# Sparse attention and SoLU feed-forward in one kernel: the hand-written step order laid out anew, with the inverse sums moved from GpSimd to VectorE

## The chip, the cores and the metric

One core of a Trainium2 chip runs one program. The metric is the device time of one launch in microseconds; of the kernel before three runs are shown (below). The profile is of one further execution.

## The reference

```
scores = (q @ k.T) / sqrt(64)                  # 8 batches x 8 heads, 576 x 576, head_dim 64
kth    = 32nd largest score of each row
attn   = softmax(scores where scores >= kth), else 0
x      = attn @ v                              # heads side by side: 4608 tokens x 512
h      = x @ w_in                              # 4608 x 1024
solu   = h * softmax(h)
ln     = (solu - mean) / sqrt(var + 1e-6) * g_ln
out    = ln @ w_out                            # 4608 x 512
```

q, k, v are float32; w_in and w_out come as float64 and are turned into float32 on the chip.

## The kernel before

The work is cut into 32 **pairs** (one batch, two heads). A pair has nine **tiles** j of 128 rows x 576 scores: two heads times four blocks of 128 queries, and one tile for the last 64 queries of both heads. Tokens are cut into 36 tiles of 128 (four per batch, and one of the 64-token rests of two batches).

The exact 32nd largest score is found by counting. First, moments of the scores are worked out without the scores: `prep_t`, `prep_m` transpose q and k on TensorE, `prep_tc`, `prep_mc` copy them out on ScalarE (ACT), `moments` and `spread` are small bf16 products, `spread_v` and `spread_r` (VectorE, DVE) multiply and reduce them, `first_p` (GpSimd, POOL) takes a root, `first` (DVE) makes a first threshold t0. Then `scores` (L747, PE) makes the scores of the query block t, `evac` (L758, ACT) brings a tile to SBUF as X, `count0` (L766, DVE) counts the scores over t0, `second` (L774 to L781, DVE) corrects the threshold, `count1` (L789, ACT) counts again, `third` (L798 to L806, DVE) corrects again, `count2` (L821, ACT) counts and keeps the signs `sg`. In the next step of the plan the same pair is finished: `nearest` (L842, L846, DVE) finds the eight scores next to the threshold, `kth` (L859 to L874, DVE) picks the 32nd, `exps` (L853, ACT) takes exponentials E of three tiles at a time, `keep` (L883, DVE) masks one tile of E and sums it, `inverse` inverts three sums, `norm` (L898, POOL) scales one tile, `transpose_p` (L909, PE) and `transpose_last` (L929, PE) transpose it, `copy_p` (L923, ACT) and `copy_last` copy it out, `attn_v` (L958, PE) multiplies by v in three parts, `copy_v` (ACT) copies that out.

A token tile goes through `mm1` (L982, PE), `hmax` (L991, DVE), `hexp` (ACT), `solu` (DVE), `square` (ACT), `ln` (POOL), `transpose_ln` (PE), `copy_ln` (ACT), `mm2` (L1046, PE) and `store`. One of them is worked on beside each pair, a second one in three of the steps.

**What sets the order.** Every engine takes its instructions strictly in the order in which they are written. That order is made by a table: `at(time, f, ...)` gives each piece a planned time, the list is sorted by it, and each piece then adds its instructions to its engines' queues. The planned times only sort; no engine waits for a clock. A pair's plan is shifted by `STEP` from pair to pair. The first 18 `weights_step` pieces turn the weights into float32, mostly on POOL and DVE.

**Buffers.** `ps_big` has two buffers (two banks each), taken in turn by h of `mm1`, y of `spread` and the scores; `ps_tp` has two, for all transposes; `ps_o` has two, for `spread`'s tail, `attn_v` and `mm2`. X has six buffers of three tiles, three to a pair, so pair i+2 writes where pair i had its scores: `evac` of tiles 0 to 2 of pair i+2 waits for `keep` of tiles 0 to 2 of pair i, and so on by threes. In time, `keep` of pair i, the counts of pair i+1 and `evac` of pair i+2 follow each other in one step.

Of the kernel before, what the change touches and what calls it, by code (L numbers as in the profile page):

```python
# [443 lines left out]
def fast_path(  # L444
# [612 lines left out]


    todo = []
    STEP = 40.0  # L1060

    def at(time, f, *args):
        todo.append((time, len(todo), f, args))

    def pair_times(i):
        b = i * STEP
        if i == 0:
            at(b - 40, load_qk, 0)
        else:
            at(b - 30, load_qk, i)  # L1070
# [2 lines left out]
        at(b - 18.0, prep_t, i)
        at(b - 17.4, prep_m, i, "q")
        at(b - 13.9, prep_tc, i)
        at(b - 13.6, prep_mc, i, "q")
        at(b - 13.5, prep_m, i, "k")
        at(b - 13.0, prep_mc, i, "k")
        at(b - 12.9, moments, i)
        at(b - 12.4, moments_c, i)  # L1080
        at(b - 12.2, spread, i)
        at(b - 9.6, spread_v, i)
        at(b - 8.8, spread_r, i)
        at(b - 5.0, first_p, i)
        at(b - 2.5, first, i)

        for t in range(NM + 1):
            at(b - 2.6 + 1.75 * t, scores, i, t)
        for j in range(NT):
            at(b - 1.3 + 0.875 * j, evac, i, j)  # L1090
            at(b - 0.6 + 0.875 * j, count0, i, j)
            at(b + 9.0 + 0.78 * j, count1, i, j)
            at(b + 19.9 + 0.78 * j + (1.5 if j > 3 else 0), count2, i, j)
        at(b + 7.4, second, i)
        at(b + 16.6, third, i)

        b += STEP
        for g, t in enumerate((7.4, 16.8, 18.3)):
            at(b + t, exps, i, g)
            at(b + 8.35 + 4.35 * g, side, i, g)  # L1100
            at(b + 26.0 + 2.6 * g, inverse, i, g)
        at(b + 21.5, kth, i)
        for j in range(NT):
            at(b + 8.4 + 1.45 * j, nearest, i, j)
            at(b + 23.0 + 0.8 * j, keep, i, j)
            at(b + 27.0 + 0.78 * j + 0.2 * (j // 3), norm, i, j)
            at(b + 28.0 + 0.85 * j, transpose_p, i, j)
            at(b + 28.7 + 0.85 * j, copy_p, i, j)
        for part, t in enumerate((31.2, 34.6, 35.4)):
            at(b + t, transpose_last, i, part)  # L1110
            at(b + t + 0.6, copy_last, i, part)
            at(b + t + 1.2, attn_v, i, part)
        at(b + 38.0, copy_v, i, 1)
        at(b + 39.0, copy_v, i, 2)

    def token_times(n, x, stores):

        d = {"x": x, "stores": stores}
        late = n > NPAIR
# [3 lines left out]
        at(b + 13.9, hmax, d)
        at(b + 15.8, hexp, d)
        at(b + 17.2, solu, d)
        at(b + 22.2, square, d)
        at(b + 23.6, ln, d)
# [97 lines left out]
```

## Time and profile before

| | before |
|---|---|
| three runs, median (lowest to highest) | 2001.91 us (1997.06 to 2002.42) |
| the profiled execution | 1995.56 us, span 1993.4 us |
| mean granted TensorE clock | 0.831 of 2.4 GHz |
| busy: PE, DVE, ACT, POOL | 1426.5, 1219.6, 1178.4, 659.3 us |

No engine is busy for more than 72% of the span, so shares of busy time do not say what a step costs. The steps have to be looked at one by one: `second` runs once per pair and marks their beat, and within a step the waits show which engine is behind which.

### The profile page before, as it was taken

To read this page: it belongs to the slowest core of one execution; us is meant where nothing else is said; L and a number is where in the kernel's file an instruction comes from. 1 tells how busy PE (TensorE), PEld (TensorE's weight loads), DVE (VectorE), ACT (ScalarE), POOL (GpSimd) and SP (SyncE) were. 2 spreads that over 40 slices of the span, in tenths; PEclk is the share of its full clock that TensorE was granted. 3 is DMA by queue.
4 is the path that set the end of the run, shared out by engine and by line. 5 is a ranking of instruction groups with operands and counts; after the bars stand their busy time and mean duration, and the time that the engine had idled before them with its cause. 6 is when DMAs were issued, how large, how long until landed. Compare 5 with 4: busy or idle time off the path is not lost.

```text
span 1993.4 us, 21797 instructions
## 1 busy us (share of the span) xinstructions
PE 1426.5 (72%) x7043; PEld 793.5 (40%) x7043; DVE 1219.6 (61%) x2784; ACT 1178.4 (59%) x2398; POOL 659.3 (33%) x806
## 2 busy tenths in 40 slices
PE   5254156777777788877777789777777788776797
PEld 3122033444444444444444445444444444443443
DVE  3745756666667766466677656467776666578411
ACT  5443465666666666466666665566667665576321
POOL 4557542333333222333332223333222333332301
PEclk9986577788878898888887888788888888888899
DMA  3111100000000000000000000100000000000000
GB/s 82 39 43 50 38 24 19 18 25 25 24 19 24 24 13 24 24 24 25 19 23 25 18 19 18 29 24 19 24 19 20 23 19 25 24 12 12 6 14 20
DMA packets 101899, 48.68 MB, mean 24 GB/s; under 512 B 86921, under 2 KB 95121, under 8 KB 101777
## 3 DMA queue, kind: packets, MB, share of 16 engines
q1 hardware_dynamic: 101776, 47.21, 8.8%
q8 instruction: 58, 0.95, 0.2%
q14 instruction: 65, 0.52, 0.1%
HBM read 37.75 MB, written 9.44 MB: 24 GB/s over the span
## 4 chain that ended last, share of the span: by engine, by line
DVE 40%; PE 37%; ACT 10%; POOL 5%; issue 5%; DMA 2%; SPq 0%; DVEq 0%; POOLq 0%; ACTq 0%
PE s_ps L747 11%; DVE w L842 10%; DVE w L846 10%; DVE E L883 9%; PE om L958 8%; PE tp_p L909 6%; ACT X L758 5%; PE h_ps L982 3%; PE o_ps L1046 3%; PE tp_pt L929 3%; POOL E L898 2%; DVE hmax L991 2%; DVE solu L1006 2%; POOL rden L894 1%; PE ot L958 1%
## 5 line engine op out<-in xcount | busy, mean ns | idle before, releaser
L766 DVE TENSOR_SCALAR_CACHE_REDUCE junkv<-X,t 128x576 bf16<-128x576 f32 x288 | 224.9, 810 | 297.0 <-ACT X L758 295.6
L909 PE MATMUL tp_p<-ident,E 128*128 128x128 f32 x1152 | 248.8, 369 | 207.0 <-POOL E L898 200.6
L923 ACT COPY PT<-tp_p 128x512 f32<-128x512 f32 x256 | 146.3, 587 | 375.7 <-PE tp_p L909 375.3
L747 PE MATMUL s_ps<-qkT 64*128 64x288 f32 (+1 forms) x1280 | 293.2, 493 | 44.4 <-ACT X L758 43.6
L758 ACT ACTIVATE X<-s_ps 128x576 f32<-128x576 f32 x288 | 179.5, 651 | 183.0 <-PE s_ps L747 163.3
L909 PEld LDWEIGHTS tp_p<-ident,E 128*128 128x128 f32 x1152 | 172.6, 186 | 280.1 <-POOL E L898 247.4
L814 POOL TENSOR_SCALAR tt<-t 128x9 f32<-128x9 f32 x32 | 7.5, 233 | 781.2 <-DVE al L830 778.7
L898 POOL TENSOR_SCALAR E<-E,rden 128x576 f32<-128x576 f32 x288 | 260.0, 920 | 9.7
L1046 PE MATMUL o_ps<-w_out,lnT 128*128 128x512 f32 x576 | 254.9, 595 | 1.0 <-ACT lnT L1041 1.0
L883 DVE SCALAR_TENSOR_TENSOR E<-X,kth,E 128x576 f32<-128x576 f32 x288 | 245.6, 917 | 1.4
L842 DVE SCALAR_TENSOR_TENSOR w<-X,al,sg 128x576 f32<-128x576 f32 x288 | 235.4, 817 | 3.4
L821 ACT ACTIVATE sg<-X,t 128x576 bf16<-128x576 f32 x288 | 220.1, 766 | 17.7 <-DVE t L806 13.2
L789 ACT ACTIVATE junka<-X,t 128x576 bf16<-128x576 f32 x288 | 218.7, 766 | 14.5 <-DVE al L830 7.3
L982 PE MATMUL h_ps<-w_in,xTm 128*128 128x512 f32 x512 | 225.4, 593 | 0.0
L846 DVE MAX8 w<-w 128x8 f32<-128x576 f32 x288 | 219.2, 761 | 9.9
L747 PEld LDWEIGHTS s_ps<-qkT 64*128 64x128 f32 (+1 forms) x1280 | 151.5, 199 | 168.2 <-ACT X L758 139.1
L633 PE MATMUL tp_qk<-ident,km 128*128 128x128 f32 x128 | 35.6, 434 | 254.4 <-ACT qkT L623 254.4
L1046 PEld LDWEIGHTS o_ps<-w_out,lnT 128*128 128x128 f32 x576 | 109.3, 191 | 136.9 <-issue 128.8
L853 ACT ACTIVATE E<-X 128x1728 f32<-128x1728 f32 x96 | 154.1, 1639 | 0.0
L722 DVE TENSOR_TENSOR t<-mean,zs 128x9 f32<-128x9 f32 x32 | 5.4, 169 | 237.0 <-POOL zs L712 237.0
L982 PEld LDWEIGHTS h_ps<-w_in,xTm 128*128 128x128 f32 x512 | 95.3, 191 | 109.1 <-issue 109.1
L958 PE MATMUL om<-PT,vm 128*64 128x256 f32 x1024 | 132.3, 403 | 0.0
(115 smaller groups left out, 1759.0 us busy)
## 6 DMA issues: line engine op xcount, KB each, us to landing
qm<-in_q_dram SPq DMA_DIRECT2D x32, 256.0 KB, 3.3
km<-in_k_dram SPq DMA_DIRECT2D x32, 256.0 KB, 3.3
vm<-in_v_dram SPq DMA_DIRECT2D x32, 256.0 KB, 2.7
out_dram<-osb SPq DMA_DIRECT2D x32, 256.0 KB, 2.3
w_raw<-in_moe_w_in_dram SPq DMA_DIRECT2D x8, 512.0 KB, 4.0
w_raw<-in_moe_w_out_dram SPq DMA_DIRECT2D x8, 512.0 KB, 3.4
qt<-in_q_dram SPq DMA_DIRECT2D x32, 32.0 KB, 2.2
kt<-in_k_dram SPq DMA_DIRECT2D x32, 32.0 KB, 2.8
```

The costliest lines, as they stand in the source:

```text
L747: nc.tensor.matmul(out=s[:, half, 0:SH], lhsT=qkT[hd, 0, qs], rhs=qkT[hd, 1, half * SH : (half + 1) * SH], start=True, stop=True,)
L758: nc.scalar.activation(out=x_of(i, j).rearrange("p (a s) -> p a s", a=2), in_=d.pop(("s", j))[:, :, 0:SH], func=AF.Copy, scale=scale,)
L766: nc.vector.tensor_scalar(out=junk, in0=x_of(i, j), scalar1=d["t0"][:, j : j + 1], scalar2=None, op0=ALU.is_ge, op1=ALU.add, accum_out=d[" ...
L821: nc.scalar.activation(out=d["sg", j], in_=x_of(i, j), func=AF.Sign, scale=-(1.0 + 2.0**-23), bias=d["t2"][:, j : j + 1], accum_out=d["n2" ...
L842: nc.vector.scalar_tensor_tensor(out=w, in0=x_of(i, j), scalar=d["al"][:, j : j + 1], in1=d.pop(("sg", j)), op0=ALU.subtract, op1=ALU.mult,)
L846: nc.vector.max(d["w8"][:, j, :], w)
L883: nc.vector.scalar_tensor_tensor(out=e, in0=x_of(i, j), scalar=d["kth"][:, j : j + 1], in1=e, op0=ALU.is_ge, op1=ALU.mult, accum_out=den_a ...
L898: nc.gpsimd.tensor_scalar(out=e, in0=e, scalar1=st[i]["rden"][:, j : j + 1], scalar2=1.0, op0=ALU.mult, op1=ALU.mult,)
L909: nc.tensor.transpose(tp[:, c, :], p_of(i, j)[:, c * P : (c + 1) * P], ident)
L958: nc.tensor.matmul(out=o[h * D : (h + 1) * D, :], lhsT=vm[:, h, c, :] if c < NM else vt[:, h, :], rhs=rhs[0:ks, c, :], start=(c == 0), sto ...
L982: nc.tensor.matmul(out=h[:, half, :], lhsT=x[:, c, :], rhs=w_in[:, c, half * 512 : (half + 1) * 512], start=(c == 0), stop=(c == NP - 1),)
L1046: nc.tensor.matmul(out=d["o"], lhsT=d["lnT"][:, c, :], rhs=w_out[:, c, :], start=(c == 0), stop=(c == NF - 1),)
```

## The change

The constant tile `minus1` goes. `inverse` becomes an addition and a reciprocal on DVE instead of an addition and a power on POOL. `STEP` is 38 for 40, and the planned times are new throughout:

- `scores` of the next pair stand among the transposes and the products with v of the pair before, not behind all of them; `evac` accordingly stands among `copy_p`.
- `spread_v`, `spread_r` and `first` of the next pair stand among the `keep` of the pair before, not behind them; `first_p` stands ahead of the nine `norm`.
- `transpose_ln` and `copy_ln` of a token tile stand in the step of its `ln`, ahead of the scores, not in the next step behind them.
- The extra token tile of two batches has its `mm1` behind `mm2` of the regular one, 14.7 planned units later than that one's.

```diff
     def inverse(i, g):
         js = slice(3 * g, 3 * g + 3)
         rden = st[i]["rden"][:, js]
-        nc.gpsimd.tensor_scalar(
-            out=rden, in0=den_all[:, i, js], scalar1=1e-9, scalar2=1.0, op0=ALU.add, op1=ALU.mult
-        )
-        nc.gpsimd.tensor_tensor(out=rden, in0=rden, in1=minus1.broadcast_to([P, 3]), op=ALU.pow)
+        nc.vector.tensor_scalar(
+            out=rden, in0=den_all[:, i, js], scalar1=1e-9, scalar2=None, op0=ALU.add
+        )
+        nc.vector.reciprocal(rden, rden)
...
-    STEP = 40.0
+    STEP = 38.0
...
-        at(b - 9.6, spread_v, i)
-        at(b - 8.8, spread_r, i)
-        at(b - 5.0, first_p, i)
-        at(b - 2.5, first, i)
+        at(b - 10.5, spread_v, i)
+        at(b - 9.7, spread_r, i)
+        at(b - 9.0, first_p, i)
+        at(b - 6.5, first, i)
...
-            at(b - 2.6 + 1.75 * t, scores, i, t)
+            at(b - 9.0 + 1.8 * t, scores, i, t)
...
-            at(b - 1.3 + 0.875 * j, evac, i, j)
+            at(b - 7.5 + 0.9 * j, evac, i, j)
...
-            at(b + 28.0 + 0.85 * j, transpose_p, i, j)
-            at(b + 28.7 + 0.85 * j, copy_p, i, j)
+            at(b + 32.2 + 0.95 * j, transpose_p, i, j)
+            at(b + 32.8 + 0.95 * j, copy_p, i, j)
```

In the rows of the changed kernel's order below, lines are two lower than before (`scores` L745, `evac` L756 and so on).

TensorE, one step from the transposes of a pair to the token products. Before (`tp_pt` is `transpose_last`, `om` and `ot` are `attn_v`, `s_ps` is `scores`, `h_ps` and `o_ps` are `mm1` and `mm2`):

```order
L909 MATMUL tp_p<-ident,E 128x128 x16
L929 MATMUL tp_pt<-ident,E 64x128 x4
L909 MATMUL tp_p<-ident,E 128x128 x8
L958 MATMUL om<-PT,vm 64x256 x8
L958 MATMUL om<-PT,vt 64x256 x2
```

The first products with v follow here, then the rest of the transposes, all other products with v, and only then:

```order
L958 MATMUL ot<-PTt,vm 64x64 x8
L958 MATMUL ot<-PTt,vt 64x64 x2
L747 MATMUL s_ps<-qkT 128x288 x16
L747 MATMUL s_ps<-qkT 64x288 x4
L1034 MATMUL tp_ln<-ident,solu 128x128 x8
L982 MATMUL h_ps<-w_in,xTm 128x512 x8
L1046 MATMUL o_ps<-w_out,lnT 128x512 x8
```

All 20 instructions of the scores stood behind the last product with v. The same place in the changed kernel:

```order
L1032 MATMUL tp_ln<-ident,solu 128x128 x8
L745 MATMUL s_ps<-qkT 128x288 x8
L907 MATMUL tp_p<-ident,E 128x128 x4
L745 MATMUL s_ps<-qkT 128x288 x4
L907 MATMUL tp_p<-ident,E 128x128 x8
L745 MATMUL s_ps<-qkT 128x288 x4
L907 MATMUL tp_p<-ident,E 128x128 x4
L927 MATMUL tp_pt<-ident,E 64x128 x4
L907 MATMUL tp_p<-ident,E 128x128 x4
L745 MATMUL s_ps<-qkT 64x288 x4
L956 MATMUL om<-PT,vm 64x256 x8
L956 MATMUL om<-PT,vt 64x256 x2
```

Two of the five blocks of scores now stand ahead of the first transpose, the others between transposes, the last ahead of the first product with v.

ScalarE in the changed kernel, the same place (`X<-s_ps` is `evac`, `PT<-tp_p` is `copy_p`):

```order
L643 ACTIVATE qkT,mom<-tp_qk 128x512
L660 COPY mom<-tp_m 128x64
L1039 COPY lnT<-tp_ln 128x512 x2
L756 ACTIVATE X<-s_ps 128x576 x3
L921 COPY PT<-tp_p 128x4x128
L756 ACTIVATE X<-s_ps 128x576
L921 COPY PT<-tp_p 128x4x128
L756 ACTIVATE X<-s_ps 128x576
L921 COPY PT<-tp_p 128x4x128
L756 ACTIVATE X<-s_ps 128x576
L921 COPY PT<-tp_p 128x4x128
L756 ACTIVATE X<-s_ps 128x576
```

From the fourth `evac` on each stands behind a `copy_p`; before, all nine stood in one run behind the copies.

VectorE between `kth` and the counts (`yq`, `mean` and `ss` are `spread_v` and `spread_r`, `E,den_all` is `keep`, `rden` is `inverse`). Before:

```order
L874 SCALAR_TENSOR_TENSOR kth<-kth 128x9
L883 SCALAR_TENSOR_TENSOR E,den_all<-X,kth,E 128x576 x9
L692 TENSOR_TENSOR yq<-y_ps,qm 128x512
L695 TENSOR_SCALAR mean<-y_ps 128x8
L692 TENSOR_TENSOR yq<-y_t,qm 128x64
L695 TENSOR_SCALAR mean<-y_t 128x1
L703 TENSOR_REDUCE ss<-yq 128x9
```

In the changed kernel:

```order
L872 SCALAR_TENSOR_TENSOR kth<-kth 128x9
L690 TENSOR_TENSOR yq<-y_ps,qm 128x512
L693 TENSOR_SCALAR mean<-y_ps 128x8
L690 TENSOR_TENSOR yq<-y_t,qm 128x64
L693 TENSOR_SCALAR mean<-y_t 128x1
L881 SCALAR_TENSOR_TENSOR E,den_all<-X,kth,E 128x576
L701 TENSOR_REDUCE ss<-yq 128x9
L881 SCALAR_TENSOR_TENSOR E,den_all<-X,kth,E 128x576 x3
L889 TENSOR_SCALAR rden<-den_all 128x3
L892 RECIPROCAL rden<-rden 128x3
```

The first `keep` now stands behind `spread_v`, which needs the next pair's moments from PE and ACT.

## Rows read from the trace of the kernel before

**Rows 1.** The page: span, busy time, and the chain that ended last.

```profile
span 1993.4 us, 21797 instructions
PE 1426.5 (72%) x7043; PEld 793.5 (40%) x7043; DVE 1219.6 (61%) x2784; ACT 1178.4 (59%) x2398; POOL 659.3 (33%) x806
DVE 40%; PE 37%; ACT 10%; POOL 5%; issue 5%; DMA 2%; SPq 0%; DVEq 0%; POOLq 0%; ACTq 0%
```

**Rows 2.** Windows: busy time and count by engine, granted clock, DMA share, GB/s.

```profile
62.50:279.00 216.50, 83.66 (x525) 51.31 (x525) 126.62 (x284) 98.10 (x201) 125.42 (x113) 0.75 0.14 42
279.00:1808.20 1529.20, 1163.20 (x5865) 648.44 (x5866) 995.70 (x2281) 982.97 (x2010) 464.18 (x602) 0.83 0.08 21
...
1808.20:1993.40 185.20, 142.66 (x507) 71.31 (x505) 71.44 (x149) 65.92 (x121) 40.81 (x52) 0.89 0.04 12
...
951.70:1006.50 54.80, 41.15 (x216) 23.11 (x215) 36.60 (x84) 36.17 (x75) 17.00 (x22) 0.84 0.09 22
...
778.70:841.70 63.00, 50.83 (x243) 28.26 (x242) 36.45 (x84) 37.99 (x79) 16.94 (x22) 0.86 0.09 23
```

**Rows 3.** Waits over the span: who for whom, total, times, longest.

```profile
ACT PT L923 <- PE tp_p L909: 375.3, 211, 18.3
DVE junkv L766 <- ACT X L758: 295.6, 156, 15.2
```

**Rows 4.** Timeline of DVE and POOL from `keep` on, one step.

```profile
1028.19 0.82 DVE L883 SCALAR_TENSOR_TENSOR E<-X,kth,E 128x576 f32<-128x576 f32 x1
1028.93 0.08 DVE L883 DVE_READ_ACCUMULATOR E<-X,kth,E 128x1 f32 x1
...
1030.63 1.31 POOL L894 TENSOR_TENSOR rden<-rden,minus 128x3 f32<-128x3 f32 x1
1032.04 3.72 POOL L898 TENSOR_SCALAR E<-E,rden 128x576 f32<-128x576 f32 x3
1032.63 1.29 DVE L883 SCALAR_TENSOR_TENSOR E<-X,kth,E 128x576 f32<-128x576 f32 x1
1036.00 0.75 DVE L703 TENSOR_REDUCE ss<-yq 128x9 f32<-128x576 f32 x1
1037.09 2.20 POOL L898 TENSOR_SCALAR E<-E,rden 128x576 f32<-128x576 f32 x3
```

**Rows 5.** Timeline of PE in the same step: transposes, products, scores.

```profile
1034.60 2.33 PE L909 MATMUL tp_p<-ident,E 128*128 128x128 f32 x8
1043.99 1.09 PE L909 MATMUL tp_p<-ident,E 128*128 128x128 f32 x8
...
1046.84 1.95 PE L958 MATMUL om<-PT,vm 128*64 128x256 f32 x16
1049.30 0.69 PE L958 MATMUL ot<-PTt,vm 128*64 128x64 f32 x16
1050.17 1.24 PE L747 MATMUL s_ps<-qkT 64*128 64x288 f32 x8
1054.31 7.75 PE L747 MATMUL s_ps<-qkT 64*128 64x288 f32 x24 [0.27 <-ACT X L758]
```

**Rows 6.** Groups of instructions: busy us, mean ns, idle before.

```profile
L821 ACT ACTIVATE sg<-X,t 128x576 bf16<-128x576 f32 x288 | 220.1, 766 | 17.7 <-DVE t L806 13.2 <-DVE w L842 4.5
L758 ACT ACTIVATE X<-s_ps 128x576 f32<-128x576 f32 x288 | 179.5, 651 | 183.0 <-PE s_ps L747 163.3 <-ACT X L758 19.0
L853 ACT ACTIVATE E<-X 128x1728 f32<-128x1728 f32 x96 | 154.1, 1639 | 0.0
L923 ACT COPY PT<-tp_p 128x512 f32<-128x512 f32 x256 | 146.3, 587 | 375.7 <-PE tp_p L909 375.3
```

**Rows 7.** Windows of one step by stage, columns as in rows 2.

```profile
1027.00:1038.00 11.00, 5.29 (x37) 3.44 (x36) 9.65 (x26) 4.04 (x11) 7.71 (x9) 0.50 0.16 37
1038.00:1050.20 12.20, 11.87 (x95) 7.76 (x95) 0.34 (x2) 5.32 (x10) 6.74 (x10) 0.86 0.08 17
1054.30:1060.00 5.70, 5.69 (x18) 3.05 (x18) 3.30 (x9) 2.46 (x4) 0.00 (x0) 0.56 0.00 0
```

More of the change, by code (lines that the diff above doesn't have):

```diff
@@ L504, in fast_path @@
     nc.gpsimd.memset(phalf, 0.5)
-    minus1 = const.tile([P, 1], F32, tag="minus1", name="minus1")
-    nc.gpsimd.memset(minus1, -1.0)
     ones = const.tile([P, 1], F32, tag="ones", name="ones")
@@ L1066, in pair_times @@
         b = i * STEP
[L1067 to L1070, printed above, removed]
+        at(b - 32, load_qk, i)
         at(b + 1, load_v, i)
[L1073 to L1081, printed above, removed]
@@ L1082, in pair_times @@
-        at(b - 9.6, spread_v, i)
-        at(b - 8.8, spread_r, i)
-        at(b - 5.0, first_p, i)
-        at(b - 2.5, first, i)
+        at(b - 17.0, prep_t, i)
+        at(b - 16.4, prep_m, i, "q")
+        at(b - 13.0, prep_tc, i)
+        at(b - 12.8, prep_mc, i, "q")
+        at(b - 12.7, prep_m, i, "k")
+        at(b - 12.2, prep_mc, i, "k")
+        at(b - 12.1, moments, i)
+        at(b - 11.7, moments_c, i)
+        at(b - 11.5, spread, i)
+        at(b - 10.5, spread_v, i)
+        at(b - 9.7, spread_r, i)
@@ L1087, in pair_times @@
+        at(b - 9.0, first_p, i)
+        at(b - 6.5, first, i)
         for t in range(NM + 1):
-            at(b - 2.6 + 1.75 * t, scores, i, t)
+            at(b - 9.0 + 1.8 * t, scores, i, t)
         for j in range(NT):
-            at(b - 1.3 + 0.875 * j, evac, i, j)
[L1091 to L1095, printed above, removed]
+            at(b - 7.5 + 0.9 * j, evac, i, j)
+            at(b - 2.0 + 0.77 * j, count0, i, j)
+            at(b + 6.4 + 0.77 * j, count1, i, j)
+            at(b + 17.7 + 0.77 * j + (1.5 if j > 3 else 0), count2, i, j)
@@ L1097, in pair_times @@
+        at(b + 5.2, second, i)
+        at(b + 14.3, third, i)
         b += STEP
-        for g, t in enumerate((7.4, 16.8, 18.3)):
+        for g, t in enumerate((4.8, 14.6, 16.1)):
             at(b + t, exps, i, g)
-            at(b + 8.35 + 4.35 * g, side, i, g)
-            at(b + 26.0 + 2.6 * g, inverse, i, g)
-        at(b + 21.5, kth, i)
+            at(b + 6.2 + 4.26 * g, side, i, g)
+            at(b + 30.2 + 2.25 * g, inverse, i, g)
+        at(b + 23.0, kth, i)
         for j in range(NT):
-            at(b + 8.4 + 1.45 * j, nearest, i, j)
-            at(b + 23.0 + 0.8 * j, keep, i, j)
-            at(b + 27.0 + 0.78 * j + 0.2 * (j // 3), norm, i, j)
-            at(b + 28.0 + 0.85 * j, transpose_p, i, j)
-            at(b + 28.7 + 0.85 * j, copy_p, i, j)
@@ L1109, in pair_times @@
-        for part, t in enumerate((31.2, 34.6, 35.4)):
+            at(b + 6.3 + 1.42 * j, nearest, i, j)
+            at(b + 27.9 + 0.75 * j, keep, i, j)
+            at(b + 31.2 + 0.9 * j, norm, i, j)
+            at(b + 32.2 + 0.95 * j, transpose_p, i, j)
+            at(b + 32.8 + 0.95 * j, copy_p, i, j)
+        for part, t in enumerate((35.5, 39.2, 40.5)):
             at(b + t, transpose_last, i, part)
             at(b + t + 0.6, copy_last, i, part)
-            at(b + t + 1.2, attn_v, i, part)
@@ L1113, in pair_times, with token_times @@
-        at(b + 38.0, copy_v, i, 1)
-        at(b + 39.0, copy_v, i, 2)
-    def token_times(n, x, stores):
+        for part, t in enumerate((36.8, 40.6, 42.4)):
+            at(b + t, attn_v, i, part)
+        at(b + 43.0, copy_v, i, 1)
+        at(b + 43.8, copy_v, i, 2)
+    def token_times(n, x, stores, more=0.0):
         d = {"x": x, "stores": stores}
         late = n > NPAIR
-        b = (NPAIR + 1) * STEP + 15.0 * (n - NPAIR - 1) if late else n * STEP
-        c = b + 15.0 if late else b + STEP
+        b = (NPAIR + 1) * STEP + 6.0 + 15.0 * (n - NPAIR - 1) if late else n * STEP + more
@@ L1122, in token_times @@
         at(b + 6.5, mm1, d)
[L1123 to L1127, printed above, removed]
+        at(b + 14.0, hmax, d)
+        at(b + 15.4, hexp, d)
+        at(b + 17.5, solu, d)
+        at(b + 20.5, square, d)
+        at(b + 22.0, ln, d)
+        lt, c = (28.7, 30.0) if late else (27.2, STEP + 13.7 - more / 2)
         for g in range(2):
-            at(c + (13.7 if late else 5.7) + 0.3 * g, transpose_ln, d, g)
-            at(c + (13.8 if late else 6.4) + 0.4 * g, copy_ln, d, g)
@@ L1131, in token_times @@
-        at(c + 14.3, mm2, d)
-        at(c + 21.5, store, d)
+            at(b + lt + 0.3 * g, transpose_ln, d, g)
+            at(b + lt + 0.6 + 0.4 * g, copy_ln, d, g)
+        at(b + c, mm2, d)
+        at(b + c + 7.3, store, d)
     def batch_times(b):
@@ L1142, in batch_times @@
         if b % 2 == 1:
+            last = b == B - 1
             token_times(
-                n + NM if b == B - 1 else n + NM - 0.5, lambda: xs["t", b // 2],
+                n + NM - (not last), lambda: xs["t", b // 2],
                 [
@@ L1148, in batch_times @@
                 ],
+                0.0 if last else 14.7,
             )
-    at(-11.0, load_g)
+    at(-10.0, load_g)
     at(-14.0, load_w, 0)
     for n in range(len(w_chunks) + 2):
-        at(11.0 + 9.7 * n, weights_step, n)
+        at(11.0 + STEP / 4 * n, weights_step, n)
     for i in range(NPAIR):
```

## The prediction

> **What bounds the kernel now.** I read the page first: no engine is busy for more than 72% of the span, and the chain that ended last runs 40% on DVE, 37% on PE and 10% on ACT [rows 1]. So no single engine's work sets the time; a loop through several does. The windows give its beat: from the fifth `second` at 279.0 to the last at 1808.2 lie 27 steps, 1529.2 us, 56.6 each; a plain one is 54.8, with DVE busy 36.60, ACT 36.17, PE 41.15 and POOL 17.00 of it, and one with an extra token tile 63.0 [rows 2]. Every engine has 13 us or more of slack in each step. Where it lies the waits tell: ACT waits 375.3 us for transposes, DVE 295.6 us in `count0` for `evac` [rows 3]. In a step, DVE works through `nearest`, `kth` and `keep` while PE has little to do; then PE transposes and multiplies by v while DVE stands; then PE makes scores, ACT takes them out and DVE counts at that pace. Three stages in a row, DVE, then PE, then PE with ACT, and only the last of them feeds the next `nearest`. The reader should see in rows 7 that DVE is busy 0.34 of the 12.20 us of the middle stage.
>
> **The change, part by part.**
>
> *Scores among the transposes.* The step is no longer scores behind products behind transposes. I follow the new order from the end of `spread_v` (time 0) until the next one, each engine in its own order, first with the durations of full clock.
>
> (a) To the last `evac`. The first one needs the X buffer that three `keep` release; `ss` stands among them: 3 x 0.74 (start to start) + 0.75 [rows 4] = 3.0. Two `evac` of 0.65 [rows 6], the rest of the second block of scores (three quarters of it must wait for the second `evac`; a block is 1.24 [rows 5], so with some overlap 0.8), the first transpose 0.55 (1.09 for two [rows 5]) and 0.25 more until the first `norm`: 5.9. The fourth `evac` stands behind the first `copy_p` (0.59 [rows 6]) and behind the sixth `keep`, which releases its buffer at about 7.0: 7.6. Then score rest 0.85, transpose 0.55, `copy_p` 0.6, `evac` 0.65, `copy_p` 0.6, `evac` 0.65: 11.5. Score rest 0.85, transpose 0.55, and on ACT `copy_p`, `evac`, `copy_last`, `copy_p`, `evac` (3.1): 16.0. PE has the last block done at 15.4, then the first product with v, 2.46 (1046.84 to 1049.30 [rows 5]), which is 17.9; the transpose behind it, its copy, and the last `evac` 0.65: **19.7**.
>
> (b) To `count1`. Four more copies with one wait for `transpose_last`, 2.7, end at 22.4, then `exps` 1.6 [rows 6]; meanwhile PE goes through the second product from 21.6 to 24.1 and the last one, 0.87 (1049.30 to 1050.17 [rows 5]), to 25.0, and `copy_v` ends at **25.2**. DVE has done the last `count0` and `second` by 21.4.
>
> (c) `count1`, `exps`, `hexp`, `exps`, `count2`, `square`, `store`, the copies of `prep` and of the moments stand in one run on ACT. ACT's 36.17 a step [rows 2], less nine `evac` (179.5/32 = 5.6), the copies of transposes (5.2 and 1.4 for the rests), one `exps` 1.6 and four smaller copies (2.0), is 20.4; with 1.1 for gaps (an estimate) 21.5: 46.7.
>
> (d) `spread` and `spread_v`, estimated at 1.6 from their place in the step before (0.4 and 0.3 of matmuls, then 0.9 on DVE): **48.3**, and the loop closes. It is a loop of ACT and PE now. DVE has 36.60 + 1.2 for the reciprocals, and 3 for contention (below), 41 in all; it waits some 7 us at `spread_v`, with nine `keep` queued behind it. That is the wait the change adds, and POOL's `norm`, PE's transposes and the release of X wait for those nine; without it the 3.0 at the head of (a) would be over by time 0, and the loop up to 3 us shorter.
>
> *The clock.* PE's granted clock was 0.50 from 1027 to 1038, in the stretch where PE was busy 5.29 of 11.00 us, 0.86 in the denser one after it, and 0.56 in most of the scores [rows 7]. 0.50 is 1.2 GHz, 1.0 is 2.4. At the low level the transposes of two tiles took 2.33 for 1.09, three blocks of scores 7.75 for 3 x 1.24 [rows 5]. If the whole of (a) ran at it, four score rests gain 0.8 each and five transposes 0.6: 6.4, and the loop is 54.7. The new stage mixes scores, transposes and waits for ACT as the half-clock stretches of before do, but the tail of (d) and the products with v are dense. I take half of the surcharge: **51.5**, between the bounds 48.3 and 54.7.
>
> The Trainium skill speaks against the change here ("TensorE: Matmul & The Clock Gate", section "HAM oscillation — how this bites in real kernels"): short bursts of matmuls with idle time between them let the gate fall back, and each burst again starts at the lower rate. By that rule all of (a) would run at 1.2 GHz and the loop would be 54.7; the trace agrees with 0.50 and 0.56 for two such stretches, not with 0.86 for the third.
>
> *Inverse sums on DVE.* POOL loses an addition and a power per three tiles; the first power took 1.31 beside `keep` [rows 4]. The third `keep` ends 0.74 after 1028.93 and the first `norm` starts at 1032.04 [rows 4], 2.4 later. Now a `keep` more stands ahead, and two small DVE instructions of about 0.2 each. Three pairs cost DVE 1.2 a step, hidden in its 7 us of waiting; POOL's 17.00 falls by about 4, which nothing waits for. If DVE's cover were gone the price is 1.2 a step.
>
> *`norm` beside more of DVE's work.* Three `norm` took 3.72 beside `keep` and 2.20 alone; `keep` took 1.29 beside `norm` and 0.82 alone [rows 4]. Up to six `keep` run beside `norm`: 6 x 0.48 = 2.9, in the 41 above, off the path but for the release of X, where 7.0 has it. `norm` at 1.24 each keeps ahead of the transposes, which come every 1.5 to 3 us.
>
> *Token pieces.* `transpose_ln` and `copy_ln` move a step ahead into PE's wait for `moments` and `spread`; I cost them at nothing, since PE's scores wait for `keep` until 3.0. The extra token tile (three steps) holds a `ps_big` buffer that the scores need until its `solu`; it cost some 12 us before (63.0 and its neighbour, over 54.8 each [rows 2]) and I leave it at that. The loads of q and k keep their place between those of v and the store on SP, and q and k are there 20 us ahead.
>
> *The weights.* In the three steps from 62.5 to 279.0 the work on the weights has POOL busy 125.42 of 216.50 [rows 2]; that stays. I take 3.3 a step from the new order, 10, with bounds 0 and 21. *The end*, 185.2 [rows 2], is PE's token products; ahead of them the last pair's `nearest` no longer waits as long for `hmax`: 8, from 0 to 10.
>
> **The sum.** 27 x 51.5 + 36 (three extra tiles) = 1426.5, which is 102.7 less than 1529.2; with 10 and 8, 121. The profiled execution took 1995.56; the median of the runs is 2001.91, 0.3% above it. 1995.56 - 121 = 1874.6, and 0.3% more: **1881**.
>
> **The rivals.**
>
> *The clock takes it back.* All of (a) at 1.2 GHz: 27 x 54.7 + 36 = 1513, 16 less; with the 18 of weights and end 1961, as a median **1968**. For it: rows 7 and the rule. Against it: products and scores that stand close together were at 0.86. Chance 0.16.
>
> *The clock stays up.* 48.3: 27 x 48.3 + 36 = 1340, 189 less; with 18, as a median **1794**. For it: scores now fill the gaps between transposes. Chance 0.17.
>
> *Slower.* The low level lasts through the products with v as well: their 2.46, 2.46 and 0.87 double on the path of (a) and (b), 54.7 + 5.8 = 60.5, 27 x 60.5 + 36 = 1670, 140 more, as a median **2124**. It decides once the surcharge of a step is over 7.7 us ((1529.2 + 18 - 36)/27 = 56.0 against 48.3). Against it: the same products ran at full clock behind transposes before (1.95 us [rows 5]). Chance 0.07.
>
> *No change.* DVE's run of `nearest`, `kth`, `keep` still stands ahead of the transposes, and `keep` now waits for `spread_v`, so what PE no longer costs behind the transposes is lost ahead of them: about **2002**. Against it: (c) leaves DVE 7 us. Chance 0.05.
>
> **How the numbers follow.** The forecast has 0.55. Faster by over 0.3% (what these runs can tell from no change, since they spread that far): 0.55 + 0.16 + 0.17 = 0.88; same 0.05; slower 0.07. The range 1780 to 1975 takes in both clock cases and leaves out the last two and a margin at the fast end.
>
> **What would show it.** Right: `second` every 50 to 53 us; ACT with hardly an idle microsecond from `count1` to the moments; DVE's longest wait at `yq`, 5 to 8 us a step; ACT's wait for transposes well under 375; the granted clock between 0.6 and 0.9 from `spread_v` to the products. Wrong: a wait of `evac` for `keep`, or of `keep` for POOL, larger than those; `norm` late for the transposes; or a clock at one level throughout (a).

## The result, and the profile after

| | before | changed kernel |
|---|---|---|
| median (lowest to highest), 4 runs each | 2001.29 us (1997.06 to 2002.42) | 1855.62 us (1852.51 to 1857.31) |
| ratio, 95% interval | | 0.9274 (0.9255 to 0.9293) |
| span of the profiled execution, granted clock | 1993.4 us, 0.831 | 1853.2 us, 0.821 |

The changed kernel is faster by 145.7 us; 1881 had been forecast. The page after, against [rows 1]:

```profile
span 1853.2 us, 21831 instructions
PE 1478.1 (80%) x7043; PEld 822.0 (44%) x7043; DVE 1258.0 (68%) x2976; ACT 1159.3 (63%) x2398; POOL 554.0 (30%) x613
PE 48%; ACT 33%; DVE 11%; POOL 3%; DMA 2%; issue 2%; SPq 0%; DVEq 0%; ACTq 0%; POOLq 0%
```

DVE's share of the chain that ended last fell from 40% to 11%, ACT's rose from 10% to 33%: the loop now runs through PE and ACT. Windows of the changed kernel, cut at the second, fifth and last `second`, then one plain step (no extra token tile), the next, two stretches of the first one's head, and two stretches of the next one's; columns and counterparts in [rows 2]:

```profile
63.50:253.00 189.50, 91.46 (x473) 54.43 (x474) 131.51 (x300) 91.79 (x195) 111.02 (x94) 0.59 0.16 47
253.00:1682.20 1429.20, 1203.02 (x5872) 671.34 (x5870) 1024.89 (x2448) 968.45 (x2012) 383.95 (x441) 0.83 0.09 23
1682.20:1853.20 171.00, 146.67 (x556) 73.81 (x553) 75.47 (x161) 67.69 (x126) 32.13 (x40) 0.93 0.05 15
1204.40:1254.20 49.80, 41.81 (x218) 23.46 (x215) 37.80 (x91) 35.57 (x75) 13.96 (x16) 0.86 0.10 25
1254.20:1307.10 52.90, 45.62 (x217) 25.59 (x215) 37.92 (x90) 35.59 (x75) 13.95 (x16) 0.81 0.09 23
...
1228.00:1239.40 11.40, 10.24 (x53) 6.86 (x53) 8.77 (x26) 5.05 (x12) 6.16 (x6) 0.50 0.23 52
1239.40:1248.90 9.50, 7.67 (x45) 4.57 (x44) 7.40 (x20) 5.63 (x11) 5.66 (x7) 0.99 0.01 2
...
1285.00:1289.00 4.00, 3.17 (x13) 2.04 (x14) 3.93 (x12) 1.47 (x4) 3.82 (x5) 0.80 0.01 2
1289.00:1293.00 4.00, 4.00 (x12) 2.16 (x12) 3.93 (x11) 0.90 (x2) 4.00 (x5) 0.50 0.00 0
```

The 27 steps take 1429.2 for 1529.2, the three weights steps 189.5 for 216.5, the end 171.0 for 185.2. Nearly all plain steps take 49.8 to 51.2 or 53.0 to 53.2, with the same instructions in the same order. PE's timeline of two steps shows why (start, duration, engine, line, operation, tiles, shape, count, idle before). In the step of 49.8 the head runs at half clock until 1239.4 and at full clock from there; in the one of 52.9 the clock falls a second time:

```profile
1230.62 1.97 PE L1032 MATMUL tp_ln<-ident,solu 128*128 128x128 f32 x8
1232.51 2.29 PE L745 MATMUL s_ps<-qkT 64*128 64x288 f32 x8
1235.54 2.83 PE L745 MATMUL s_ps<-qkT 64*128 64x288 f32 x8 [0.73 <-ACT X L756]
...
1241.80 1.09 PE L907 MATMUL tp_p<-ident,E 128*128 128x128 f32 x8
...
1285.09 1.77 PE L745 MATMUL s_ps<-qkT 64*128 64x288 f32 x8 [0.74 <-ACT X L756]
1287.60 1.11 PE L907 MATMUL tp_p<-ident,E 128*128 128x128 f32 x4 [0.74 <-POOL E L896]
1288.65 3.58 PE L745 MATMUL s_ps<-qkT 64*128 64x288 f32 x8
1292.16 1.97 PE L907 MATMUL tp_p<-ident,E 128*128 128x128 f32 x8
```

The same two transposes take 1.09 and 1.97, a block of scores 1.77 (at 1285.09) and 3.58. The difference of the two steps, 53.0 - 49.8 = 3.2, is half of the 6.4 that the prediction gave to the whole head. The steps of 51.0 lie between the two in their granted clock as well (0.83). The two waits of [rows 3], both shorter now, and the one that the change added:

```profile
ACT PT L921 <- PE tp_p L907: 336.0, 150, 8.7
DVE junkv L764 <- ACT X L756: 232.2, 116, 4.1
DVE yq L690 <- PE y_ps L672: 130.7, 28, 6.8
```

DVE's new wait at `spread_v` is 130.7 / 28 = 4.7 us a step. A third wait shrank most, PE's for POOL's `norm`, before and in the changed kernel:

```profile
PE tp_p L909 <- POOL E L898: 200.6, 63, 17.4
...
PE tp_p L907 <- POOL E L896: 35.9, 16, 7.7
```

ACT's timeline of the step of 49.8 shows the last wait of the head and the start of `count1`:

```profile
1234.84 1.19 ACT L756 ACTIVATE X<-s_ps 128x576 f32<-128x576 f32 x2 [1.63 <-PE s_ps L745]
...
1252.13 0.59 ACT L921 COPY PT<-tp_p 128x512 f32<-128x512 f32 x1 [2.92 <-PE tp_p L907]
1252.62 0.66 ACT L756 ACTIVATE X<-s_ps 128x576 f32<-128x576 f32 x1
1258.89 0.78 ACT L787 ACTIVATE junka<-X,t 128x576 bf16<-128x576 f32 x1
```

### The profile page after: what moved, and what is told of

It reads as the page before. It is cut to its first block, busy times and chain, and to the rows that moved or that the text cites. A ratio compares the mean times of both kernels' runs of the same rounds, so it can differ in the third digit from the quotient of the medians.

```text
span 1853.2 us, 21831 instructions
## 1 busy us (share of the span) xinstructions
PE 1478.1 (80%) x7043; PEld 822.0 (44%) x7043; DVE 1258.0 (68%) x2976; ACT 1159.3 (63%) x2398; POOL 554.0 (30%) x613
## 4 chain that ended last, share of the span: by engine, by line
PE 48%; ACT 33%; DVE 11%; POOL 3%; DMA 2%; issue 2%; SPq 0%; DVEq 0%; ACTq 0%; POOLq 0%
PE s_ps L745 15%; ACT junka L787 8%; ACT sg L819 8%; PE om L956 8%; PE tp_p L907 7%; PE h_ps L980 6%; PE o_ps L1044 6%; ACT PT L921 4%; ACT E L851 3%; ACT X L756 3%; DVE E L881 3%; PE tp_pt L927 2%; DVE w L840 2%; DVE w L844 2%; PE tp_ln L1032 2%
## 5 line engine op out<-in xcount | busy, mean ns | idle before, releaser
L745 PE MATMUL s_ps<-qkT 64*128 64x288 f32 (+1 forms) x1280 | 384.4, 607 | 87.9 <-ACT X L756 55.6
L764 DVE TENSOR_SCALAR_CACHE_REDUCE junkv<-X,t 128x576 bf16<-128x576 f32 x288 | 222.9, 808 | 233.0 <-ACT X L756 232.2
L921 ACT COPY PT<-tp_p 128x512 f32<-128x512 f32 x256 | 147.4, 591 | 336.0 <-PE tp_p L907 336.0
L745 PEld LDWEIGHTS s_ps<-qkT 64*128 64x128 f32 (+1 forms) x1280 | 196.2, 255 | 233.0 <-ACT X L756 135.0
L896 POOL TENSOR_SCALAR E<-E,rden 128x576 f32<-128x576 f32 x288 | 272.6, 965 | 16.6 <-DVE rden L892 14.0
L756 ACT ACTIVATE X<-s_ps 128x576 f32<-128x576 f32 x288 | 186.1, 657 | 145.2 <-PE s_ps L745 111.9
L881 DVE SCALAR_TENSOR_TENSOR E<-X,kth,E 128x576 f32<-128x576 f32 x288 | 260.9, 937 | 0.2
L907 PE MATMUL tp_p<-ident,E 128*128 128x128 f32 x1152 | 219.8, 334 | 50.4 <-POOL E L896 35.9
L907 PEld LDWEIGHTS tp_p<-ident,E 128*128 128x128 f32 x1152 | 154.3, 168 | 143.8 <-POOL E L896 75.7
L956 PE MATMUL om<-PT,vm 128*64 128x256 f32 x1024 | 124.6, 385 | 0.0
L690 DVE TENSOR_TENSOR yq<-y_ps,qm 128x512 f32<-128x512 f32 x32 | 22.1, 691 | 140.2 <-PE y_ps L672 130.7
```

Of the source, the lines that this page charges most:

```text
L745: nc.tensor.matmul(out=s[:, half, 0:SH], lhsT=qkT[hd, 0, qs], rhs=qkT[hd, 1, half * SH : (half + 1) * SH], start=True, stop=True,)
L756: nc.scalar.activation(out=x_of(i, j).rearrange("p (a s) -> p a s", a=2), in_=d.pop(("s", j))[:, :, 0:SH], func=AF.Copy, scale=scale,)
L881: nc.vector.scalar_tensor_tensor(out=e, in0=x_of(i, j), scalar=d["kth"][:, j : j + 1], in1=e, op0=ALU.is_ge, op1=ALU.mult, accum_out=den_a ...
L896: nc.gpsimd.tensor_scalar(out=e, in0=e, scalar1=st[i]["rden"][:, j : j + 1], scalar2=1.0, op0=ALU.mult, op1=ALU.mult,)
L907: nc.tensor.transpose(tp[:, c, :], p_of(i, j)[:, c * P : (c + 1) * P], ident)
L956: nc.tensor.matmul(out=o[h * D : (h + 1) * D, :], lhsT=vm[:, h, c, :] if c < NM else vt[:, h, :], rhs=rhs[0:ks, c, :], start=(c == 0), sto ...
```

## The experiments

Each ran three rounds beside the kernel before, which took 1994 us in all of them and 2001 beside the changed kernel; so runs are compared by their ratios to it, given in brackets with the 95% interval. "Plain steps" are those without an extra token tile; "like steps" are those of two kernels that both have, or both lack, a long second low stretch of the clock. Line shifts are left out of the diffs.

**The two parts of the change alone.** `pow_back` is the changed kernel with the inverse sums on GpSimd again, `recip_alone` the kernel before with them on VectorE (its diff; `pow_back` has the reverse, and the tile `minus1` again):

```diff
-        nc.gpsimd.tensor_scalar(out=rden, ..., scalar1=1e-9, scalar2=1.0, op0=ALU.add, op1=ALU.mult)
-        nc.gpsimd.tensor_tensor(out=rden, in0=rden, in1=minus1.broadcast_to([P, 3]), op=ALU.pow)
+        nc.vector.tensor_scalar(out=rden, ..., scalar1=1e-9, scalar2=None, op0=ALU.add)
+        nc.vector.reciprocal(rden, rden)
```

> The new order with inverse put back on GpSimd (an addition and a power, as before). Theory A, the step is a loop of ACT and PE: the first norm comes some 2 us later than its present start, of which the first transpose has 1 us to spare, so about 1 us a step is lost: 1865 to 1895 us, against 1856 for the changed kernel. Theory C, the gain came from the sums' move to VectorE: more than half of it goes back, over 1930 us.

> The kernel before with nothing changed but inverse, on VectorE. In the old order the norms and the inverse sums of a pair stand in one run on GpSimd ahead of the transposes, and the three powers with their additions take some 4.5 us of it, so theory A has 1 to 3 us a step to gain: 1905 to 1970 us against 2001. Theory C has most of the whole gain here: under 1890 us. If the norms alone set the pace: 1990 to 2005.

| | time | ratio to before (95%) | weights steps / 27 steps / end | plain steps |
|---|---|---|---|---|
| before | 1994 | | 217 / 1529 / 185 | 54.8 to 55.2, 57.1 to 57.5 |
| new order, sums on GpSimd (`pow_back`) | 1937.81 | 0.9723 (0.9706 to 0.9739) | 191 / 1502 / 179 | 53.0 to 53.2, 54.1 to 55.8 |
| old order, sums on VectorE (`recip_alone`) | 1923.26 | 0.9631 (0.9595 to 0.9667) | 215 / 1462 / 181 | 52.0 to 52.8, 54.6 |
| both (the changed kernel) | 1855.62 | 0.9274 (0.9255 to 0.9293) | 190 / 1429 / 171 | 49.8 to 51.2, 53.0 to 53.2 |

By the ratios the order alone gives 2.8% (56 us), the sums alone 3.7% (71 us), the two together 7.3%: they nearly add up. `pow_back` came out in the range of theory C, `recip_alone` in that of theory A. By the columns of the 27 steps the sums, which the prediction costed at nothing, have 67 to 72 of the 100 us gained there and the order 28 to 33, whichever is put in first; the order has 25 more in the weights steps. The two waits that shrank in the changed kernel [rows 3] are longer than before in `pow_back`, so the new order by itself did not shorten them:

```profile
ACT PT L923 <- PE tp_p L909: 423.9, 146, 10.3
DVE junkv L766 <- ACT X L758: 369.0, 178, 4.1
```

PE's wait for `norm` over the span is 200.6 before, 145.3 in `recip_alone`, 95.7 in `pow_back` and 35.9 with both. POOL's timeline in `pow_back` shows where the sums stand in the new order:

```profile
1000.64 0.70 POOL L708 TENSOR_SCALAR zs<-ss 128x9 f32<-128x9 f32 x1 [6.37 <-DVE ss L703]
1001.42 2.24 POOL L712 TENSOR_TENSOR zs<-zs,phalf 128x9 f32<-128x9 f32 x1
...
1004.04 0.82 POOL L891 TENSOR_SCALAR rden<-den_all 128x3 f32<-128x3 f32 x1
1004.94 1.31 POOL L894 TENSOR_TENSOR rden<-rden,minus 128x3 f32<-128x3 f32 x1
1006.36 2.01 POOL L898 TENSOR_SCALAR E<-E,rden 128x576 f32<-128x576 f32 x2
```

And PE's, beside it:

```profile
1002.92 1.77 PE L747 MATMUL s_ps<-qkT 64*128 64x288 f32 x8 [0.74 <-ACT X L758]
1007.69 1.11 PE L909 MATMUL tp_p<-ident,E 128*128 128x128 f32 x4 [3.00 <-POOL E L898]
```

`first_p`, the sum, the power and the first `norm` follow each other on POOL, and PE stands 3.00 us for that `norm`. In the changed kernel POOL goes from `first_p` straight to `norm`, and PE's wait at the same place (1287.60, behind the block at 1285.09 above) is 0.74. The first transpose starts 4.77 after the second block of scores here (1002.92 to 1007.69) and 2.51 after it there: 2.3 of the 2.7 to 3.2 us by which like steps differ.

`inverse_early` asks what the place of the sums is worth in the old order:

```diff
-            at(b + 26.0 + 2.6 * g, inverse, i, g)
+            at(b + 25.1 + 2.4 * g, inverse, i, g)
```

> The kernel before with the inverse sums on VectorE (recip_alone, 1923 us), and each inverse right behind its third keep instead of one or two keep later; nothing else. It asks what of the 74 us between recip_alone and scores_spread_back (1850) is this place. A: the first norm starts one keep (0.8 us) earlier and the whole chain of norms, transposes and scores with it: 0.6 to 0.9 us a step, 20 to 30 us, 1893 to 1905. B: the place is worth nothing, since the norms run behind each other and the last of them comes no earlier: 1918 to 1928; the rest lies in the other differences of that layout (weights earlier, moments and token pieces in other places).

It took 1956.87 (0.9816, 0.9797 to 0.9835): neither branch, but 33.6 slower than `recip_alone`. Like steps are about as long as there (52.9 for 52.0 to 52.8, and 54.6 in both); but here nearly all plain ones are 54.6, there six. PE's timeline of such a step, from the second block of scores on:

```profile
1036.71 1.89 PE L747 MATMUL s_ps<-qkT 64*128 64x288 f32 x8 [0.73 <-ACT X L758]
1038.87 7.74 PE L747 MATMUL s_ps<-qkT 64*128 64x288 f32 x24 [0.27 <-ACT X L758]
```

And the third block in a step of 52.0 in `recip_alone`, whose later blocks stay at full clock:

```profile
1010.83 1.77 PE L747 MATMUL s_ps<-qkT 64*128 64x288 f32 x8 [0.27 <-ACT X L758]
```

Branch B's reason held for the work (the first `norm` came 0.6 earlier, the last 0.2 later, counted from `second`); the rest is the second low stretch. In like steps the sums are worth some 2.4 us a step in the old order (54.8 to 52.4, 57.2 to 54.6). The mix of step lengths moved the whole kernel by 1.8% here (0.9816 - 0.9631), half of what `recip_alone` gained, so the 71 and 56 us above are those of these layouts and carry an uncertainty of that size.

**The interleaving.** `scores_back` puts the scores, `evac` and `count0` of the changed kernel back into one run behind the last product with v (`second`, two `copy_v` and one `exps` are shifted with them):

```diff
-            at(b - 9.0 + 1.8 * t, scores, i, t)
+            at(b + 4.5 + 0.3 * t, scores, i, t)
-            at(b - 7.5 + 0.9 * j, evac, i, j)
-            at(b - 2.0 + 0.77 * j, count0, i, j)
+            at(b + 4.65 + 0.15 * j, evac, i, j)
+            at(b + 4.75 + 0.15 * j, count0, i, j)
```

> The changed kernel with scores, evac and count0 put back into one run behind the last product with v; all else as changed. Theory A: the ten microseconds and more of scores stand in the loop again while the transposes are no faster than their norms; 4 to 6 us a step more, 1950 to 2030 us. Theory C: the interleaving is worth little, under 1890 us.

It took 2100.15 (1.0532, 1.0515 to 1.055), slower than the kernel before and than every expectation: steps of 61.4. Here `keep` still stands behind `spread_v`, so moments, `keep`, `norm`, transposes, products and scores all follow one another. `scores_spread_back` also takes that away:

```diff
-            at(b - 10.5, spread_v, i)
-            at(b - 9.7, spread_r, i)
-            at(b - 9.0, first_p, i)
-            at(b - 6.5, first, i)
+            at(b - 3.9, spread_v, i)
+            at(b - 3.8, spread_r, i)
+            at(b - 0.2, first_p, i)
+            at(b - 0.1, first, i)
-            at(b + 30.2 + 2.25 * g, inverse, i, g)
+            at(b + 29.7 + 2.25 * g, inverse, i, g)
```

(and `norm` 0.9 earlier).

> scores_back, and spread_v, spread_r, first_p and first put back behind the nine keep and the norms, as in the kernel before; the sums on VectorE stay. In scores_back a step took 61.4 us, 8 more than the old order with the same sums (recip_alone). If what makes it so is that keep stands behind spread_v and the norms behind first_p while the scores no longer need them early: 52 to 55 us a step, 1890 to 1970 us. If the rest of the new order is to blame (copies, exps, token pieces): still over 2050 us.

It took 1849.88 (0.9279, 0.9264 to 0.9295), faster than either range and the time of the changed kernel by the ratios, with steps of 51.4 (53.7 with a second low stretch) and weights steps, 27 steps and end of 205, 1411 and 170. So interleaving the scores buys nothing that a serial order does not reach with the sums on VectorE: it pays back what putting `spread_v` ahead of `keep` costs. What gives this kernel another 73 us over `recip_alone` was not taken apart further; `inverse_early` shows that moving the sums forward is not enough for it.

**The head of the loop.** `keep_first` puts the first three `keep` and their sum ahead of `spread_v`:

```diff
-            at(b + 27.9 + 0.75 * j, keep, i, j)
+            at(b + (26.0 + 0.2 * j if j < 3 else 27.9 + 0.75 * j), keep, i, j)
-            at(b + 30.2 + 2.25 * g, inverse, i, g)
+            at(b + (26.9 if g == 0 else 30.2 + 2.25 * g), inverse, i, g)
```

> The changed kernel with the first three keep and the first inverse put ahead of spread_v, into VectorE's wait of 4 to 5 us for it. The three keep release the X buffers and the first norm can start earlier. Theory A, with the scores' start (token transposes and the first block at half clock) as what sets the head of the loop: 0 to 1 us a step, 1825 to 1856 us. Theory B, VectorE's wait with nine keep queued behind it is what the step now pays for: 3 us a step, 1760 to 1775 us.

1838.65 (0.923, 0.9208 to 0.9252), about 0.5% under the changed kernel and in theory A's range. `keep_ln` is that, with `transpose_ln` and `copy_ln` behind the first block of scores:

```diff
-        lt, c = (28.7, 30.0) if late else (27.2, STEP + 13.7 - more / 2)
+        lt, c = (28.7, 30.0) if late else (29.5, STEP + 13.7 - more / 2)
-            at(b + lt + 0.6 + 0.4 * g, copy_ln, d, g)
+            at(b + lt + (0.6 if late else 2.0) + 0.4 * g, copy_ln, d, g)
```

> As keep_first, and the token tile's transposes and copies moved from ahead of the first block of scores to behind it. Theory A: the scores start 1.9 us earlier and X is free by then; 1.5 to 2.5 us a step, 1785 to 1815 us. Theory B: no more than keep_first.

1784.39 (0.8953, 0.8938 to 0.8968), at the fast end of theory A's range. PE's timeline of its head:

```profile
1028.89 3.08 PE L745 MATMUL s_ps<-qkT 64*128 64x288 f32 x8
1031.90 1.97 PE L1032 MATMUL tp_ln<-ident,solu 128*128 128x128 f32 x8
...
1035.61 0.66 PE L907 MATMUL tp_p<-ident,E 128*128 128x128 f32 x4
```

The scores start right behind `spread`, where the changed kernel first spends 1.97 on `transpose_ln` at half clock; that piece now fills the 0.73 that PE waited for `evac`. The first transpose, 0.66, is already at full clock, 6.7 us after `spread`; in the changed kernel it takes 1.11 at 1238.30, 7.6 after. Nearly all plain steps are 48.2 to 49.2.

**The clock.** `warm` is meant to fill PE's wait for ACT's copies ahead of the moments: the transposes of q are made seven times over.

```diff
-        for c in range(NM):
+        for c in list(range(NM)) * (7 if nm == "q" else 1):
```

> The changed kernel with the four transposes of q repeated six times over (same tile, same values), in the 4 us in which PE waits for ACT. Theory A with the clock as a term of its own: the clock does not fall to half in that wait, and the token transposes, the first two blocks of scores and the first transpose take 1.5 to 3 us less a step: 1765 to 1815 us. If buffers and ACT set that stretch whatever the clock: 1850 to 1860 us. If the clock falls all the same the repeats outlast the wait: 1870 to 1920 us.

1874.03 (0.9393, 0.9377 to 0.9409), slower than without. Windows from the repeated transposes on, columns as above:

```profile
1289.60:1293.20 3.60, 3.56 (x31) 3.24 (x30) 3.36 (x9) 3.60 (x10) 1.74 (x3) 1.00 0.23 79
1293.20:1295.00 1.80, 0.11 (x1) 0.11 (x2) 0.20 (x1) 1.80 (x6) 0.18 (x1) 1.00 0.02 6
1295.00:1297.30 2.30, 1.44 (x24) 1.08 (x24) 0.05 (x1) 1.75 (x6) 0.00 (x0) 0.78 0.04 9
1297.30:1305.00 7.70, 6.97 (x26) 4.48 (x24) 7.63 (x22) 2.79 (x5) 5.04 (x5) 0.50 0.35 77
1305.00:1313.00 8.00, 7.63 (x24) 4.51 (x24) 7.09 (x21) 3.54 (x7) 6.75 (x8) 0.50 0.00 0
```

The repeats filled only part of the wait: behind them PE was busy for 1.55 of 4.10 us, with waits of 1.73 and 0.86 for ACT. The clock stayed at 1.00 until 1295 and fell before 1297.30, to 0.50 over all of the head, in which PE was busy for 14.60 of 15.70 us. So the low stretch came later, and the kernel was slower. The time lies in the third range, but not for its reason, since the repeats ended before the wait did; a run that leaves PE no idle time there was not made.

**Other steps of the prediction.** `extra_early` moves the extra token tile's `mm1`, `hmax`, `hexp` and `solu` forward by 5.7 planned units, `weights_late` the weights pieces back by 3, and `attn_late` moves the first product with v behind two more transposes:

```diff
+        e = 5.7 if more else 0.0
-        at(b + 6.5, mm1, d)
+        at(b + 6.5 - e, mm1, d)
...
-        at(11.0 + STEP / 4 * n, weights_step, n)
+        at(14.0 + STEP / 4 * n, weights_step, n)
...
-        for part, t in enumerate((36.8, 40.6, 42.4)):
+        for part, t in enumerate((38.2, 40.6, 42.4)):
```

> The changed kernel with the extra token tile's first product, maximum, exponential and solu 5.7 planned units earlier, so that solu stands ahead of keep and frees the PSUM buffer before the scores want it. The trace of the changed kernel has PE wait 8 us for that solu in three steps, and scores at half clock behind it: 20 to 30 us less in all, 1826 to 1836 us. If something else is as late in those steps: 1850 to 1858 us.

1837.13 (0.9207, 0.9192 to 0.9223): some 13 to 18 less than the changed kernel, short of the 20 to 30 expected. The steps of an extra tile took 58.3, 56.0 and 54.9 for 62.6.

> The changed kernel with the weights' pieces three planned units later, which puts one of four per step between the norms, as in the kernel before; the other three stay clear of them. If the early steps gained (27 us where 10 were forecast) because the norms run unbroken: 4 to 8 us in each of some four steps is lost, 1870 to 1890 us. If they gained as all other steps did: 1850 to 1862 us.

1879.86 (0.9433, 0.9417 to 0.9449), as expected if the unbroken `norm` are the cause: the weights steps rose to 211, the rest stayed at 1431 and 171. POOL's timeline in one of them:

```profile
172.93 2.59 POOL L896 TENSOR_SCALAR E<-E,rden 128x576 f32<-128x576 f32 x2
176.15 1.07 POOL L560 TENSOR_SCALAR w_out<-w_out,g_col 128x512 f32<-128x512 f32 x1 [0.63 <-DVE w_out L52]
...
186.06 5.09 POOL L896 TENSOR_SCALAR E<-E,rden 128x576 f32<-128x576 f32 x7
```

Weights work stands between the second and the third `norm`, 10 us long; in the changed kernel the nine run in one piece.

> The changed kernel with the first product with v put behind the transposes of tiles 5 and 6 (it stood between those of tiles 4 and 5). In the trace of the changed kernel ACT waits 2.9 us for the transpose of tile 5 behind that product, and the last evac and the last count0 wait with it. Theory A: PE and ACT work side by side there, 1 to 2 us a step less: 1795 to 1830 us. If the product is only moved to where the copies wait for it: 1850 to 1860 us.

1846.21 (0.9253, 0.9237 to 0.9268): the interval overlaps with the changed kernel's, and neither range holds. The 27 steps took 1431 for 1429, plain ones mostly 51.3 (50.2 to 53.4); what was gained lies in the weights steps, 181 for 190. ACT's wait behind the product fell from 2.92 to 0.90, but its waits for transposes over the span did not (336.0 in the changed kernel, 345.3 here), and the granted clock was 0.795 for 0.821. That the clock took the gain back is argued from those numbers, not shown.

> keep_ln, extra_early and attn_late together. If the three shorten different stretches of the loop, their gains add up: 1784 less 12 to 18 for the extra tiles and what attn_late shows: 1725 to 1770 us. If they shorten the same one: 1770 to 1785 us.

`all_three` (`keep_ln`, `extra_early` and `attn_late` together) took 1752.17 (0.8784, 0.877 to 0.8799), with plain steps of 47.3 to 48.4: 5.3% under the changed kernel by the ratios (0.8784 / 0.9274), the fastest version here. It lies in the range for gains that add up: 34 us under `keep_ln`, where the other two alone had given 13 and 4 (all by the ratios).

## Why the prediction was right, and where not

**The loop and its length: right.** The walk gave 51.5 a step between 48.3 and 54.7; the 27 steps took 1429.2 for 1426.5. From the end of `spread_v` at 1231.5 the last `evac` ended at 1253.3, 21.8 on (19.7 at full clock); `count1` came 5.6 behind it (5.5); ACT's run took 20.9 in the step ahead (1209.1 to 1230.0; 21.5); moments and `spread_v` 1.5 (1.6). DVE's wait stood at `yq`, if with 4.7 for 7. PE and ACT close the loop, as the chain shows. One of its signs did not come: ACT's wait for transposes is 336.0, not "well under 375"; and though DVE's longest single wait is at `yq`, those in `count0` still add up to more (232.2 us over the span, 130.7 at `yq`).

**The clock: the size right, the picture not.** The 6.4 for all of (a) is 6.2 by its own terms (4 x 0.8 and 5 x 0.6). "Half of the surcharge" is not what every step pays: the step of 49.8 has one low stretch, that of 53.0 two, and by their granted clocks (0.86 and 0.81) some 14 and 20 us at the low level. "The clock takes it back" and "stays up" were drawn as rivals for the whole run, and the kernel lies between them.

By the rule that was cited (the Trainium skill, "TensorE: Matmul & The Clock Gate", section on HAM oscillation) idle time between bursts is what lets the clock fall. The trace agrees in part: the second fall of the longer step came while PE was busy for 3.17 of 4.00 us, waiting 0.74 at a time, and the fall in `warm` behind waits of 1.73 and 0.86. That all of (a) would be low is not what it shows: 0.99 from 1239.4 on in the step of 49.8. Nor does dense work alone mean the high level: PE was busy for 4.00 of 4.00 us at 0.50 from 1289, and in [rows 7] already for 5.69 of 5.70 at 0.56, which the prediction counted among the stretches with idle time. Its "products and scores that stand close together were at 0.86" is misread too: that stretch of [rows 7] has transposes and products, and no scores. The measurement decides.

**The inverse sums: wrong.** The step that failed is "POOL's 17.00 falls by about 4, which nothing waits for". POOL's total does not limit a step, but its first power stood in series with the first `norm`, and PE's first transpose waits for that one. [Rows 4] had half of it: the power ends at 1031.94 and the first `norm` starts at 1032.04. The other half stands in PE's timeline of the kernel before, in the same step, in a row that [rows 5] leaves out:

```profile
1033.38 3.55 PE L909 MATMUL tp_p<-ident,E 128*128 128x128 f32 x12 [4.21 <-POOL E L898]
```

PE stood 4.21 us for that `norm`. The 2.4 us between third `keep` and first `norm` were read and not followed to PE. POOL's 17.00 fell by 3.0, to 13.96 a step. In runs the sums are worth 71 us in the old order, some 37 there with the step lengths of `inverse_early`, and some 90 in the new order (0.9723 - 0.9274, of 1994).

**The source of the rest: wrong.** The whole of a step's gain was credited to the scores among the transposes. With the sums costed right, the order alone has 56 us, 25 of them in the weights steps and 7 at the end, and it lengthened the waits that the interleaving was to shorten (`pow_back`); `scores_spread_back` reaches the same total with the scores in one run. The total came out because the walk took each engine's durations in the new order, whatever had made it shorter.

**Mis-sized terms.** Weights steps: 27 for 10, since nothing stands between the `norm` any more (`weights_late` gives 22 back). The end: 14.2 for 8; both lie outside the bounds given. The extra tile: 62.6 + 56.9 is 17.5 over two plain steps of 51, not 12; three times 5.5 more explains why the plain steps could be shorter than 51.5 and the sum still hold; that the two errors, some 15 us each, cancel is luck. `transpose_ln`, "at nothing": its place is worth 55 us between `keep_first` and `keep_ln` (0.923 - 0.8953, of 1994), 1.7 a step. "Up to 3 us shorter" without DVE's wait: `keep_first` found 0.5%, since the first `evac` waited 1.63 us for scores at half clock, not for X.

## What to carry to other kernels

Follow a short instruction to the engine that waits behind it before costing it at nothing: two small operations on a lightly used engine were worth at least as much as the whole new order. When a new order and a small edit come together, run each alone, and also the new order without its main idea; here that last run matched the change. Where an engine's clock has two levels, compare steps of like level, or a change of order is judged by how the levels happen to fall.

## What the runs showed of the hardware

Steps with the same instructions in the same order ran at different lengths in one execution, 2 to 3 us apart, by how long TensorE's clock stood at its low level (0.50, 1.2 GHz). In the changed kernel the second low stretch began between 1285 and 1289, where PE was busy for 3.17 of 4.00 us with no wait longer than 0.74, and it held while PE was busy for 4.00 of 4.00 us from 1289 to 1293. Which steps have it could change from one order of small VectorE instructions to another (`recip_alone` and `inverse_early`); what decides it stays open.

Small GpSimd instructions are dear beside VectorE's work with two SBUF inputs. POOL's timeline of the changed kernel beside `keep`:

```profile
1232.97 0.71 POOL L706 TENSOR_SCALAR zs<-ss 128x9 f32<-128x9 f32 x1 [6.38 <-DVE ss L701]
1233.77 2.26 POOL L710 TENSOR_TENSOR zs<-zs,phalf 128x9 f32<-128x9 f32 x1
...
1236.41 8.65 POOL L896 TENSOR_SCALAR E<-E,rden 128x576 f32<-128x576 f32 x9
```

In `recip_alone`, away from `keep`, the same addition and root took 0.21 and 1.81. DVE's timeline in the same step of the changed kernel:

```profile
1237.08 1.30 DVE L881 SCALAR_TENSOR_TENSOR E<-X,kth,E 128x576 f32<-128x576 f32 x1
...
1240.87 0.59 DVE L889 TENSOR_SCALAR rden<-den_all 128x3 f32<-128x3 f32 x1
...
1243.77 0.81 DVE L764 TENSOR_SCALAR_CACHE_REDUCE junkv<-X,t 128x576 bf16<-128x576 f32 x1
```

`keep`, with X and E as inputs, takes 1.30 beside `norm` for 0.81 alone; `count0`, with one large input, takes its 0.81 beside the same `norm` (8.65 from 1236.41, until 1245.06). The Trainium skill ("GPSIMD Engine Reference", section 1) says that the two engines share their SBUF interfaces and get in each other's way where the VectorE instruction has two SBUF inputs; the trace agrees for these two. It does not settle the small addition, which has one such input: 0.17 at 1235.02 ahead of `norm`, and beside it 0.16 at 1238.31 but 0.59 at 1240.87.
